# Windowed attention, a rotation mixer and a gated feed-forward on one core: low parts of weights queued later, copies and taps on ScalarE, first loads by two queues

## The chip, the core and the metric

The program runs on one core of a Trainium2 chip. Its engines work side by side, each through its own list of instructions in order: TensorE (PE in the profile, its weight loads PEld), VectorE (DVE), ScalarE (ACT), GpSimd (POOL) and SyncE (SP), which issues most transfers. An instruction that needs another engine's result waits on a semaphore, and all that stands behind it on its own engine waits with it. The metric is the device time of one execution in microseconds, the median of the runs shown. The cost of the host is not in it.

## The reference

```python
# attention, 2 batches x 8 heads, 768 positions, 64 wide
scores = q @ k.T / 8 - slope[h] * dist           # dist: |i-j|, or n_local for far global columns
keep   = (j < n_global) | ((0 <= i-j) & (i-j < n_local))      # n_global 8, n_local 96
x      = softmax(where(keep, scores, -1e9)) @ v  # heads side by side: x is 2 x 768 x 512
# rotation mixer
theta  = x @ w_theta                             # 512 x 512
zr, zi = x * cos(theta), x * sin(theta)
y      = w_tok_r @ zr + w_tok_i @ zi             # 768 x 768, over the tokens
u      = x + y
x2     = u + relu(u @ w_ch)                      # 512 x 512
# gated feed-forward
h      = relu(x2 @ w_in)                         # 512 x 1024
c      = conv over tokens of h, 3 taps per channel
out    = (h * sigmoid(c)) @ w_out                # 1024 x 512
```

The six large weights arrive in 64-bit floating point, everything else in 32 bits.

## The kernel before, in words

The program first reads n_global and n_local and takes one of two branches. With these inputs it is `run_fast`, whose window fits into 128 previous columns; `run_general` is the other and is not run. `begin` issues the loads of the first pair of heads and builds the distance table before the branch; the flag that decides the branch comes out of the same VectorE work.

**Attention** goes in 48 steps, three for each of the 16 heads, two tiles of 128 query rows in a step. Step j is spread over later steps by fixed lags: scores at j on TensorE (bank S), the reduction that adds the table and takes the maximum at j+1 on VectorE (L316), two exponentials at j+2 on ScalarE (L325), transposes at j+3 (L334, bank PT), their copy to memory at j+4 on ScalarE (L101), the product with v at j+5 (bank O), the normalisation at j+6 on VectorE after each third step. After every second head the 128 new channels of x are transposed (X) and split (xTs). From about step 34 the angles of batch 0 (bank TH, tile t at a time) run between the steps.

**Weights.** A weight of 384 or 512 columns passes through six jobs that `weight` makes: a load into one of three (later five) buffers, `a` (one ScalarE operation, L117), `b` (two VectorE operations, L122 and L123), `c` (two more, L129 and L130), which make a 32-bit number of the 64 bits, `d` (the high part, a rounding copy on ScalarE, L101) and `e` (the low part, the difference, on VectorE, L109). `advance` puts the jobs of several weights into one list in an interleaved order, and `run(k)` takes the next k from it; where the calls of `run` stand in the program decides when each engine gets them. Every product is made of three: high by high, low by high, high by low.

**Mixing** follows: the angles of batch 1 (TH, S, PT), the rounding of an angle to turns (`reduce_theta`, r), sine and cosine on ScalarE and the products with x on VectorE (`trig`, z, in high and low parts), then the products with the token weights wt, first half of the 768 columns for batch 0 and 1 (from 151 us and 176 us), then the second half (from 202 us and 234 us), while the weights of the second half, w_ch and w_in are converted. `tok_end` adds a bank to x (xT), `u_split` splits the sum (us), `ch` makes u @ w_ch from 259 us, `ff_in` the product with w_in from 301 us, `gate` the taps, the sigmoid and the split g, and `ff_out` the last product from 368 us.

The code is written out in the order in which each engine takes it; no scheduler moves it.

Of the kernel before, what the change touches and what calls it, by code (L numbers as in the profile page):

```python
# [21 lines left out]
P = 128  # L22
# [31 lines left out]
class Net:  # L54
# [111 lines left out]
    def advance(self, n):  # L166
        j = self.jobs

        def put(i, *steps):
            if 0 <= i < len(j):  # L170
                self.bg.extend(j[i][x] for x in steps)

        put(n - 3, 5)
        put(n - 1, 1)
        put(n - 2, 2, 3)
        put(n, 0)
        put(n - 2, 4)
# [49 lines left out]

def pad_q(nc, t):
    nc.gpsimd.memset(t[D:P, S + KK : QK], 0.0)
    nc.vector.memset(t[0:D, 0:S], 0.0)  # L230
# [172 lines left out]
class Mix:  # L403
# [64 lines left out]
    def reduce_theta(self, th, out):  # L468
# [3 lines left out]
        nc.scalar.activation(out, th, AF.Copy, scale=1.0 / TWO_PI)  # L472
        yield
        nc.vector.tensor_scalar(t, out, MAGIC, -MAGIC, op0=ALU.add, op1=ALU.add)
        nc.vector.tensor_tensor(out, out, t, op=ALU.subtract)

    def trig(self, b, t, r, z, em, eh, el):
# [5 lines left out]
        nc.scalar.activation(r, r, AF.Sin, scale=TURN)  # L483
# [95 lines left out]
    def gate(self, b, f, h, c, banks, em, eh, el):  # L579
# [3 lines left out]
        for hf in range(2):  # L583
            nc.scalar.activation(h[:, HALF * hf : HALF * hf + HALF], banks[hf][:, 0:HALF], AF.Relu)
        yield
        nc.vector.tensor_scalar(c, h, cw[:, f, 1:2], None, op0=ALU.mult)
# [28 lines left out]
    def tail(self, early):  # L615
# [56 lines left out]
        tr = [self.trig(1, s, r[s], self.z[1][s], "VV", "VV", "VV") for s in range(NT)]  # L672
# [62 lines left out]
        for step in (n.f64_a, n.f64_b, n.f64_c):  # L735
            step(n.head["cwb"], n.head["cwt"])
        pipe = Pipe()
        pipe.step(*(self.u_split(0, x, 0, "V", "V") for x in range(KC)))
        for m in range(KC):
# [3 lines left out]
            pipe.step(*(self.u_split(0, x, 1, "V", "V") for x in range(KC) if m == 0))  # L743
# [5 lines left out]

        self.us[1] = [n.slot(t, [P, KC, S], F32R, "us") for t in ("xs0", "y1")]  # L750
# [22 lines left out]
        cs = n.slot("xT1", [P, 4, S], F32, "c")  # L773
# [3 lines left out]
        for k in range(2 * NF):  # L777
# [3 lines left out]
            pipe.step(self.gate(b, f, hs[k % 3], cs[:, k % 4], banks, "V", "A", "V"))  # L781
# [10 lines left out]
def run_fast(tc, net):  # L792
# [4 lines left out]
    att.load_v(0)  # L797
    att.load_v(1)
# [27 lines left out]
    for j in range(NJ + LAG_N + 3):  # L826
# [44 lines left out]
        net.run(1 if j == 0 else 0 if j < 4 else 1 if j < 33 else 3)  # L871
# [4 lines left out]
def run_general(tc, net):  # L876
# [3 lines left out]
    mix = Mix(net, xs)  # L880
    for i in range(NH):
# [51 lines left out]
def begin(nc, io, net, small, head):  # L933
# [6 lines left out]
    for k, q in ((slice(0, 2 * KW), slice(KK, KK + 2 * P)), (slice(2 * KW, KK), slice(KK + 2 * P, KK + S))):  # L940
        nc.sync.dma_start(qk0[0:D, S + k.start : S + k.stop], two[:, k])
        nc.sync.dma_start(qk0[D:P, S + k.start : S + k.stop], one[:, S + k.start : S + k.stop])
# [75 lines left out]
```

## Time and profile before

| | |
|---|---|
| runs of the kernel before | 438.99, 438.33 and 2325.94 us, median 438.99 |
| the profiled execution, whole | 441.24 us |
| its span, first to last instruction | 439.0 us |
| mean granted TensorE clock | 0.988 |
| busy: TensorE, VectorE, ScalarE, GpSimd | 413.4, 342.9, 203.6, 2.9 us |
| read from memory, written | 34.39 MB, 3.15 MB |

The profile gives one execution. A group line names the code line, engine, operation, what it writes and reads and its shape, then busy time, the mean time of one and the idle time before it with the engine that ended it. A bracket in a timeline row is the same for one instruction. Matmuls are pipelined: a record begins when the array takes it up and ends by a model, so the distance from one begin to the next is the better measure of pace. A granted clock of 1.00 is 2.4 GHz and 0.50 is 1.2 GHz.

### The profile page before, as it was taken

The numbers are of one execution on the slowest core, as the hardware profiler recorded it, in microseconds if no ns is written. First come the engines' busy times: TensorE is split into PE (matmuls) and PEld (weight loads), VectorE is DVE, ScalarE is ACT, GpSimd is POOL, SyncE is SP. The second block draws the span as 40 slices with busy tenths as digits, with TensorE's granted clock in tenths as the row PEclk, the third lists the DMA queues.
The fourth block names the chain that finished last, engine by engine and source line by source line (L and its number), as shares of the span: only waits on it lengthen the run. The fifth ranks groups of instructions, "written<-read, shape, count | busy, mean of one in ns | idle before, by whom it ended". The sixth has DMA issues, their size and how long they took to land.

```text
span 439.0 us, 6394 instructions
## 1 busy us (share of the span) xinstructions
PE 413.4 (94%) x2376; PEld 383.4 (87%) x2376; DVE 342.9 (78%) x783; ACT 203.6 (46%) x401; POOL 2.9 (1%) x12
## 2 busy tenths in 40 slices
PE   4799999999999999999879998699999999999995
PEld 3699999988897899999669998499999999888885
DVE  4458877977788998997879988999999999980001
ACT  2467777675668414702332233544554445530000
POOL 2000000000000000000000000000000000000000
PEclk9889999999999999999999999989999999999999
DMA  5946565372410014004454234222000000002111
GB/s 161 249 142 179 144 160 150 110 216 73 167 47 1 0 30 116 1 6 139 134 166 145 96 107 141 97 88 88 9 0 2 0 2 0 1 33 110 49 48 55
DMA packets 13096, 38.04 MB, mean 87 GB/s; under 512 B 1856, under 2 KB 2304, under 8 KB 13056
## 3 DMA queue, kind: packets, MB, share of 16 engines
q1 hardware_dynamic: 13056, 37.54, 29.1%
q8 instruction: 20, 0.33, 0.3%
q14 instruction: 20, 0.16, 0.1%
HBM read 34.39 MB, written 3.15 MB: 86 GB/s over the span
## 4 chain that ended last, share of the span: by engine, by line
PE 61%; DVE 30%; ACT 3%; DMA 2%; SPq 2%; issue 1%; ACTq 0%; DVEq 0%
PE O L112 18%; PE S L112 16%; PE TH L112 8%; PE PT L112 8%; PE X L112 5%; PE PT L334 4%; DVE wbit L129 4%; DVE wbit L130 4%; DVE z L109 3%; DVE wbit L123 3%; DMA wst<-w_theta 2%; DVE wbit L122 2%; DVE wt L109 2%; DVE z L105 2%; ACT wt L101 2%; DVE r L488 2%
## 5 line engine op out<-in xcount | busy, mean ns | idle before, releaser
L112 PE MATMUL S<-qk 128*128 128x256 f32 (+1 forms) x192 | 50.9, 394 | 6.6 <-DVE nnl L981 5.8
L316 DVE CUSTOM_DVE_ANT_0 a<-S,a 128x256 f32<-128x256 f32 (+1 forms) x96 | 34.9, 398 | 23.1 <-PE PT L334 15.7
L325 ACT ACTIVATE a<-a,nm 128x256 f32<-128x256 f32 (+1 forms) x96 | 41.4, 480 | 11.0 <-DVE nm L316 11.0
L112 PEld LDWEIGHTS S<-qk 128*128 128x128 f32 x192 | 33.8, 205 | 10.7 <-issue 7.3
L101 ACT ACTIVATE wt<-wbit 128x384 fp32r<-128x384 f32 x24 | 12.5, 523 | 52.1 <-DVE wbit L130 52.1
L112 PE MATMUL O<-wt,z 128*128 128x384 f32 x144 | 29.2, 342 | 5.3 <-ACT wt L101 5.3
L101 ACT ACTIVATE a<-PT 128x512 f32<-128x512 f32 (+1 forms) x48 | 26.6, 553 | 15.4 <-PE PT L334 15.0
L112 PEld LDWEIGHTS O<-wt,z 128*128 128x128 f32 x144 | 24.8, 188 | 7.9 <-ACT wt L101 6.5
L112 PE MATMUL O<-a,a 128*128 128x65 f32 x236 | 31.1, 276 | 0.0
L112 PEld LDWEIGHTS O<-a,a 128*128 128x128 f32 x236 | 30.2, 200 | 0.0
L334 PE MATMUL PT<-ident,a 128*128 128x128 f32 x176 | 27.9, 279 | 2.3 <-ACT a L101 2.3
L334 PEld LDWEIGHTS PT<-ident,a 128*128 128x128 f32 x176 | 22.8, 145 | 7.5 <-ACT a L101 2.7
L112 PE MATMUL PT<-wt,z 128*128 128x384 f32 x144 | 28.1, 335 | 0.0
L112 PE MATMUL S<-wt,z 128*128 128x384 f32 x144 | 26.5, 336 | 0.5 <-DVE z L109 0.5
L112 PEld LDWEIGHTS S<-wt,z 128*128 128x128 f32 x144 | 25.1, 188 | 0.8 <-DVE z L109 0.8
L112 PE MATMUL TH<-wth,xTs 128*128 128x512 f32 x96 | 25.9, 406 | 0.0
L112 PEld LDWEIGHTS PT<-wt,z 128*128 128x128 f32 x144 | 25.3, 188 | 0.0
L109 DVE TENSOR_TENSOR wt<-wbit,wt 128x384 fp32r<-128x384 f32 x24 | 13.4, 557 | 11.5 <-ACT wt L101 11.2
L117 ACT ACTIVATE wbit<-wst 128x384 f32<-128x384 f32 (+1 forms) x33 | 19.9, 602 | 4.8 <-DMA wst<-w_theta 4.8
L130 DVE SCALAR_TENSOR_TENSOR wbit<-wst,wbit 128x384 int32<-128x384 int32 (+1 forms) x33 | 20.6, 623 | 1.1
L129 DVE SCALAR_TENSOR_TENSOR wbit<-wst,wbit 128x384 int32<-128x384 int32 (+1 forms) x33 | 20.5, 622 | 0.9
L123 DVE TENSOR_SCALAR wbit<-wbit 128x512 int32<-128x512 int32 (+1 forms) x48 | 18.9, 394 | 1.6
(179 smaller groups left out, 868.6 us busy)
## 6 DMA issues: line engine op xcount, KB each, us to landing
wst<-w_tok SPq DMA_DIRECT2D x17, 384.0 KB, 3.1
a<-v SPq DMA_DIRECT2D x16, 357.5 KB, 3.9
qk<-qk SPq DMA_DIRECT2D x14, 396.0 KB, 5.5
out<-scratch SPq DMA_DIRECT2D x11, 256.0 KB, 2.0
qk<-w_tok SPq DMA_DIRECT2D x7, 384.0 KB, 3.1
wst<-w_out SPq DMA_DIRECT2D x5, 512.0 KB, 3.5
wst<-w_theta SPq DMA_DIRECT2D x4, 512.0 KB, 9.5
qk<-w_in SPq DMA_DIRECT2D x4, 512.0 KB, 3.5
```

The lines of the kernel that those rows point to most:

```text
L101: self.nc.scalar.activation(out, in_, AF.Copy)
L105: self.nc.vector.tensor_copy(out, in_)
L109: e.tensor_tensor(out, in_, hi.bitcast(F32), op=ALU.subtract)
L112: self.nc.tensor.matmul(out, l, r, start=start, stop=stop)
L117: self.nc.scalar.activation(t.bitcast(F32), w[:, 1 : w.shape[1] : 2].bitcast(F32), AF.Abs)
L122: nc.vector.tensor_scalar(t.bitcast(F32), t.bitcast(F32), F64_LOW, F64_HIGH, op0=ALU.max, op1=ALU.min)
L123: nc.vector.tensor_scalar(t, t, 3, 0x3FFFFFFF, op0=ALU.logical_shift_left, op1=ALU.bitwise_and)
L129: nc.vector.scalar_tensor_tensor(t, lo, 29, t, op0=ALU.logical_shift_right, op1=ALU.bitwise_or)
L130: nc.vector.scalar_tensor_tensor(t, hi, -(1 << 30), t, op0=ALU.bitwise_and, op1=ALU.bitwise_or)
L316: nc.vector.tensor_tensor_reduce(sS[:, c], s["sp"][:, c], self.T[i % H][:, 256:TW] if t0 else self.T[i % H][:, 0:256], scale=-0.125, scala ...
L325: self.nc.scalar.activation(sS[:, rng[u]], sS[:, rng[u]], AF.Exp, bias=nm[:, u : u + 1], scale=-1.0)
L334: self.nc.tensor.transpose(pt[:, c], sS[:, c], net.head["ident"])
```

## The change

Six things are altered; the matmuls and their order are the same on TensorE.

1. In `advance` the low part of weight n-3 is put behind the bit operations of weight n-2, where it stood ahead of them.
2. In the attention loop the first load of weights is taken at step 3, nothing more until step 9, and then two jobs in each step; before it was one at step 0, one a step from step 4, and three from step 33.
3. The loads of the first pair of heads are cut in two: three are issued by SyncE and three by ScalarE. The seventh (the second head's q, 64x768) is issued after the branch, behind the first load of v. The taps' weights (cwb) are loaded where they are needed, and their conversion stands later.
4. The rounding of an angle is a second ScalarE copy (adding the magic number) and one VectorE operation, where it was two VectorE operations. The result has the other sign, which the sine's scale undoes.
5. The rounding copies for the high part of z in batch 1 and of the first u move from VectorE to ScalarE.
6. The middle tap moves from VectorE to ScalarE, with a fifth buffer for c. The clearing of unused q rows moves from VectorE to GpSimd.

```diff
@@ advance
-        put(n - 3, 5)
         put(n - 1, 1)
         put(n - 2, 2, 3)
         put(n, 0)
+        put(n - 3, 5)
         put(n - 2, 4)
@@ load of the second head's q, and the clearing
+def load_qk_second(nc, io, t):
+    nc.sync.dma_start(t[D:P, 0:S], io["qk"][0, 1][:, 0:S])
...
-    nc.vector.memset(t[0:D, 0:S], 0.0)
+    nc.gpsimd.memset(t[0:D, 0:S], 0.0)
@@ reduce_theta
         nc.scalar.activation(out, th, AF.Copy, scale=1.0 / TWO_PI)
-        yield
-        nc.vector.tensor_scalar(t, out, MAGIC, -MAGIC, op0=ALU.add, op1=ALU.add)
-        nc.vector.tensor_tensor(out, out, t, op=ALU.subtract)
+        nc.scalar.activation(t, out, AF.Copy, bias=MAGIC)
+        yield
+        nc.vector.scalar_tensor_tensor(out, t, -MAGIC, out, op0=ALU.add, op1=ALU.subtract)
@@ gate
-        yield
-        nc.vector.tensor_scalar(c, h, cw[:, f, 1:2], None, op0=ALU.mult)
+        nc.scalar.activation(c, h, AF.Identity, scale=cw[:, f, 1:2])
+        yield
@@ tail
-        tr = [self.trig(1, s, r[s], self.z[1][s], "VV", "VV", "VV") for s in range(NT)]
+        tr = [self.trig(1, s, r[s], self.z[1][s], "VV", "AA", "VV") for s in range(NT)]
...
-        for step in (n.f64_a, n.f64_b, n.f64_c):
-            step(n.head["cwb"], n.head["cwt"])
+        self.nc.sync.dma_start(n.head["cwb"], n.io["conv_w"].bitcast(I32))
...
-        pipe.step(*(self.u_split(0, x, 0, "V", "V") for x in range(KC)))
+        pipe.step(*(self.u_split(0, x, 0, "A", "V") for x in range(KC)))
...
-            pipe.step(*(self.u_split(0, x, 1, "V", "V") for x in range(KC) if m == 0))
+            pipe.step(*(self.u_split(0, x, 1, "A", "V") for x in range(KC) if m == 0))
...
         self.tok_end(1, KC - 1, 1, last)
 
+        for step in (n.f64_a, n.f64_b, n.f64_c):
+            step(n.head["cwb"], n.head["cwt"])
@@ run_fast
     att.load_v(0)
+    load_qk_second(nc, io, att.qk[0])
     att.load_v(1)
...
-        net.run(1 if j == 0 else 0 if j < 4 else 1 if j < 33 else 3)
+        net.run(1 if j == 3 else 0 if j < 9 else 2)
@@ begin
-    for k, q in ((slice(0, 2 * KW), slice(KK, KK + 2 * P)), (slice(2 * KW, KK), slice(KK + 2 * P, KK + S))):
-        nc.sync.dma_start(qk0[0:D, S + k.start : S + k.stop], two[:, k])
-        nc.sync.dma_start(qk0[D:P, S + k.start : S + k.stop], one[:, S + k.start : S + k.stop])
-        nc.sync.dma_start(qk0[0:D, S + q.start : S + q.stop], two[:, q])
-    nc.sync.dma_start(qk0[D:P, 0:S], one[:, 0:S])
+    ks, qs = (slice(0, 2 * KW), slice(2 * KW, KK)), (slice(KK, KK + 2 * P), slice(KK + 2 * P, KK + S))
+    for e, k, q in ((nc.sync, ks[0], qs[0]), (nc.scalar, ks[1], qs[1])):
+        e.dma_start(qk0[0:D, S + k.start : S + k.stop], two[:, k])
+        e.dma_start(qk0[D:P, S + k.start : S + k.stop], one[:, S + k.start : S + k.stop])
+        e.dma_start(qk0[0:D, S + q.start : S + q.stop], two[:, q])
```

Three places of the instruction lists show it. The first is ScalarE just after the branch, steps 2 to 8 of attention; `wbit<-wst` is job `a` of a weight of w_theta, which reads the loaded buffer. Before:

```order
L325 ACTIVATE a_5_134<-a_5_134,nm_176 128x256 x2
L101 ACTIVATE a_3_132<-PT_182 128x384
L117 ACTIVATE wbit_200<-wst_146 128x512
L325 ACTIVATE a_5_134<-a_5_134,nm_189 128x128
L325 ACTIVATE a_5_134<-a_5_134,nm_189 128x256
L101 ACTIVATE a_4_133<-PT_194 128x512
L325 ACTIVATE a_5_134<-a_5_134,nm_205 128x256 x2
L101 ACTIVATE a_5_134<-PT_210 128x512
L117 ACTIVATE wbit_242<-wst_147 128x512
```

And now:

```order
L101 ACTIVATE a_4_131<-PT_193 128x512
L330 ACTIVATE a_5_132<-a_5_132,nm_202 128x256 x2
L101 ACTIVATE a_5_132<-PT_207 128x512
L330 ACTIVATE a_5_132<-a_5_132,nm_223 128x256 x2
L101 ACTIVATE a_3_130<-PT_229 128x384
L330 ACTIVATE a_5_132<-a_5_132,nm_241 128x128
L330 ACTIVATE a_5_132<-a_5_132,nm_241 128x256
L101 ACTIVATE a_4_131<-PT_246 128x512
L330 ACTIVATE a_5_132<-a_5_132,nm_259 128x256 x2
L101 ACTIVATE a_5_132<-PT_264 128x512
L117 ACTIVATE wbit_297<-wst_145 128x512
```

The first job on a weight stood behind the first copy of PT and now stands behind the sixth, with the exponentials of five more steps ahead of it.

The second is VectorE where the conversion of the second half of the token weights begins; `wt` is the low part, job `e`. Before:

```order
L122 TENSOR_SCALAR wbit_1884<-wbit_1884 128x384
L123 TENSOR_SCALAR wbit_1884<-wbit_1884 128x384
L129 SCALAR_TENSOR_TENSOR wbit_1884<-wst_148,wbit_1884 128x384
L130 SCALAR_TENSOR_TENSOR wbit_1884<-wst_148,wbit_1884 128x384
L109 TENSOR_TENSOR wt_1881<-wbit_1884,wt_1881 128x384
L122 TENSOR_SCALAR wbit_1887<-wbit_1887 128x384
```

And now:

```order
L122 TENSOR_SCALAR wbit_1883<-wbit_1883 128x384
L123 TENSOR_SCALAR wbit_1883<-wbit_1883 128x384
L129 SCALAR_TENSOR_TENSOR wbit_1883<-wst_147,wbit_1883 128x384
L130 SCALAR_TENSOR_TENSOR wbit_1883<-wst_147,wbit_1883 128x384
L122 TENSOR_SCALAR wbit_1886<-wbit_1886 128x384
L123 TENSOR_SCALAR wbit_1886<-wbit_1886 128x384
L129 SCALAR_TENSOR_TENSOR wbit_1886<-qk_63,wbit_1886 128x384
L130 SCALAR_TENSOR_TENSOR wbit_1886<-qk_63,wbit_1886 128x384
L109 TENSOR_TENSOR wt_1880<-wbit_1883,wt_1880 128x384
```

Between the last bit operation of a weight and its low part there now stand the four bit operations of the next weight.

The third is ScalarE in the second half of the angles, at the first token tiles of batch 1; abs, sine and cosine of a tile are L487 to L489 now, and `z` the new copies. Before there were none of these copies here:

```order
L482 ACTIVATE scratch<-r_145 128x512
L483 ACTIVATE r_145<-r_145 128x512
L484 ACTIVATE scratch<-scratch,hp 128x512
L482 ACTIVATE scratch<-r_145 128x512
L483 ACTIVATE r_145<-r_145 128x512
```

And now:

```order
L478 ACTIVATE scratch<-r_144 128x512
L487 ACTIVATE scratch<-r_144 128x512
L488 ACTIVATE r_144<-r_144 128x512
L489 ACTIVATE scratch<-scratch,hp 128x512
L487 ACTIVATE scratch<-r_144 128x512
L488 ACTIVATE r_144<-r_144 128x512
L489 ACTIVATE scratch<-scratch,hp 128x512
L101 ACTIVATE z_1647<-r_144 128x512
L101 ACTIVATE z_1647<-scratch 128x512
L487 ACTIVATE scratch<-r_144 128x512
```

The copies of a tile stand behind the sine and cosine of the tile after it.

## Rows read from the trace of the kernel before

**Rows 1.** The page's busy time: engine, share of the span, instructions.

```profile
PE 413.4 (94%) x2376; PEld 383.4 (87%) x2376; DVE 342.9 (78%) x783; ACT 203.6 (46%) x401; POOL 2.9 (1%) x12
```

**Rows 2.** The page's chain of waits, shares of the span by engine.

```profile
PE 61%; DVE 30%; ACT 3%; DMA 2%; SPq 2%; issue 1%; ACTq 0%; DVEq 0%
```

**Rows 3.** Waits of TensorE: for whom, us in total, times, longest.

```profile
PE O L112 <- ACT wt L101: 5.3, 4, 1.8
PE O L112 <- DVE us L109: 4.1, 2, 2.9
PE PT L334 <- ACT a L101: 2.3, 1, 2.3
PE TH L112 <- DVE xT L534: 1.1, 1, 1.1
PE S L112 <- DMA qk<-qk: 0.8, 1, 0.8
PE S L112 <- DVE z L109: 0.5, 1, 0.5
```

**Rows 4.** Windows: stretch, length, busy PE PEld DVE ACT POOL, PEclk, DMA share, GB/s.

```profile
12.10:18.90 6.80, 4.59 (x30) 3.78 (x28) 2.48 (x14) 1.81 (x5) 0.00 (x0) 1.00 1.01 266
18.90:25.70 6.80, 5.90 (x24) 5.43 (x25) 2.36 (x10) 5.22 (x13) 0.00 (x0) 0.50 0.72 192
34.08:46.73 12.65, 12.65 (x99) 11.84 (x98) 10.49 (x40) 9.87 (x23) 0.00 (x0) 1.00 0.60 155
277.60:288.75 11.15, 6.85 (x27) 5.58 (x25) 11.05 (x24) 7.59 (x17) 0.00 (x0) 0.85 0.28 96
301.40:368.60 67.20, 67.20 (x385) 67.20 (x385) 65.56 (x91) 34.80 (x60) 0.00 (x0) 1.00 0.04 12
```

**Rows 5.** Timeline of PE, 15 to 22 us: start, us, line, what, count, [idle before].

```profile
15.02 0.78 PE L112 MATMUL O<-a 128*128 128x65 f32 x6
16.63 0.89 PE L112 MATMUL S<-qk 128*128 128x128 f32 x4 [0.83 <-DMA qk<-qk]
19.80 0.90 PE L334 MATMUL PT<-ident,a 128*128 128x128 f32 x3 [2.28 <-ACT a L101]
```

**Rows 6.** Timeline of ACT in the same stretch.

```profile
17.92 0.66 ACT L117 ACTIVATE wbit<-wst 128x512 f32<-128x512 f32 x1 [4.82 <-DMA wst<-w_theta]
```

**Rows 7.** Timeline of PE at the second half's token products, 202 to 235 us.

```profile
202.13 2.24 PE L112 MATMUL O<-wt,z 128*128 128x384 f32 x12
...
206.29 2.24 PE L112 MATMUL O<-wt,z 128*128 128x384 f32 x12
...
234.50 0.68 PE L112 MATMUL S<-wt,z 128*128 128x384 f32 x3
```

**Rows 8.** Timeline of DVE there: two successive low parts.

```profile
202.83 0.56 DVE L109 TENSOR_TENSOR wt<-wbit,wt 128x384 fp32r<-128x384 f32 x1 [0.59 <-ACT wt L101]
...
205.83 0.56 DVE L109 TENSOR_TENSOR wt<-wbit,wt 128x384 fp32r<-128x384 f32 x1 [0.59 <-ACT wt L101]
```

**Rows 9.** Timeline of PE at the products with w_ch, 277 to 289 us.

```profile
277.64 2.14 PE L112 MATMUL O<-us,wch 128*128 128x384 f32 x7
...
284.64 0.62 PE L112 MATMUL O<-us,wx 128*128 128x384 f32 x2 [2.87 <-DVE us L109]
...
288.75 1.72 PE L112 MATMUL X<-us,wch 128*128 128x384 f32 x9
```

**Rows 10.** Groups by form: mean ns behind the comma; stretches from 138 to 369 us.

```profile
L474 DVE TENSOR_SCALAR scratch<-r 128x512 f32<-128x512 f32 x6 | 2.5, 419 | 0.0
L105 DVE CAST z<-r 128x512 fp32r<-128x512 f32 x12 | 5.0, 416 | 0.0
L105 DVE CAST us<-xT 128x384 fp32r<-128x384 f32 x8 | 2.3, 352 | 0.0
L586 DVE TENSOR_SCALAR c<-scratch,cwt 128x768 f32<-128x768 f32 x12 | 7.4, 616 | 0.2
L101 ACT ACTIVATE wout<-wbit 128x512 fp32r<-128x512 f32 x6 | 3.8, 628 | 8.5 <-DVE wbit L130 8.5
```

More of the change, by code (lines that the diff above doesn't have):

```diff
@@ L482, in trig @@
         nc.scalar.activation(a, r, AF.Abs)
-        nc.scalar.activation(r, r, AF.Sin, scale=TURN)
+        nc.scalar.activation(r, r, AF.Sin, scale=-TURN)
         nc.scalar.activation(a, a, AF.Sin, bias=n.head["half_pi"], scale=-TURN)
@@ L771, in tail @@
         n.drain()
-        cs = n.slot("xT1", [P, 4, S], F32, "c")
+        c4 = n.slot("xT1", [P, 4, S], F32, "c")
+        cs = [c4[:, i] for i in range(4)] + [n.slot("c", [P, S], F32, "c")]
         hs = [n.head["scratch"][:, S * i : S * i + S] for i in range(3)]
@@ L780, in tail @@
             self.ff_in(b, f, banks)
-            pipe.step(self.gate(b, f, hs[k % 3], cs[:, k % 4], banks, "V", "A", "V"))
+            pipe.step(self.gate(b, f, hs[k % 3], cs[k % 5], banks, "V", "A", "V"))
             n.run(4)
@@ L880, in run_general @@
     mix = Mix(net, xs)
+    load_qk_second(nc, io, att.qk[0])
     for i in range(NH):
@@ L939, in begin @@
     two, one = io["qk"][0, 0], io["qk"][0, 1]
-    for k, q in ((slice(0, 2 * KW), slice(KK, KK + 2 * P)), (slice(2 * KW, KK), slice(KK + 2 * P, KK + S))):
-        nc.sync.dma_start(qk0[0:D, S + k.start : S + k.stop], two[:, k])
-        nc.sync.dma_start(qk0[D:P, S + k.start : S + k.stop], one[:, S + k.start : S + k.stop])
-        nc.sync.dma_start(qk0[0:D, S + q.start : S + q.stop], two[:, q])
-    nc.sync.dma_start(qk0[D:P, 0:S], one[:, 0:S])
+    ks, qs = (slice(0, 2 * KW), slice(2 * KW, KK)), (slice(KK, KK + 2 * P), slice(KK + 2 * P, KK + S))
[3 more added lines that the diff above has]
+        e.dma_start(qk0[0:D, S + q.start : S + q.stop], two[:, q])
     pad_q(nc, qk0)
     cwb = small.tile([P, 2 * NF * 3], I32, name="cwb")
-    nc.sync.dma_start(cwb, io["conv_w"].bitcast(I32))
     R = scratch[:, 0:384]
```

## The prediction

> **What bounds the kernel now.** I read the busy time first, then the chain of waits, then what TensorE itself waited for, and last the stretches around each wait. TensorE is busy for 413.4 of 439.0 us [rows 1]. The chain of waits gives VectorE 30% of the span [rows 2], 132 us, nearly all of it in the mixer, which looks like a stage bound by VectorE. It is not quite that. In the second half's token products one token tile, four banks of six matmuls, takes from 202.13 to 206.29, 4.16 us or 173 ns a matmul [rows 7]; the stage with w_in, where TensorE has no gap in 67.20 us and issues 384 matmuls, has 175 ns [rows 4]. So TensorE runs at full pace there too, and VectorE only decides where a wait appears. The order of the matmuls is not altered, hence only gaps and time at the lower clock can be won. The reader is to see six of them in TensorE's waits, 14.1 us together [rows 3], and that pace lost around them makes them dearer than they look.
>
> **The start, 15 to 26 us.** ScalarE stands at job `a` of the first w_theta weight until 17.92, 4.82 us, for its load [rows 6]. Behind it are a copy of PT and the exponentials, and TensorE idles 2.28 us before 19.80 [rows 5]. Then the clock is at 0.50, 1.2 GHz, from 18.90 to 25.70, with TensorE busy 5.90 us in it [rows 4]; at the full level half of that, 2.95, would do. The change takes this job at step 9, when the load is there. Gain 2.28 + 2.95 = **5.2**. Just before, TensorE waits 0.83 for the second pair's q and k [rows 5]. Those loads now stand behind fewer others on SyncE (three have gone to ScalarE, the taps' weights come later), but q of the second head still goes ahead of them, into a stretch where the transfer engines are full (share 1.01, 266 GB/s) [rows 4]. Between nothing and 0.83 I take **0.5**. A new cost: ScalarE's three loads run beside the small load of n_global and n_local, from which the branch hangs. No row shows that; it is nothing if the small one goes first and at most about one wait of the kind just named, 0.83, if not. I take 0.4 lost.
>
> **Attention, steps 9 to 32.** In place of one job a step there are two, so one more weight in six steps. Six steps take 12.65 us on TensorE, VectorE is busy 10.49 and ScalarE 9.87 of it [rows 4]. A weight of 384 columns costs VectorE 3.00 us from one low part to the next, less the wait of 0.59, 2.41 [rows 8]; with 512 columns at most a third more, 3.2. VectorE then has 12.9 to 13.7 us of work for 12.65, for the two times six steps that carry the four wide weights: 0.5 to 2.1 us lost. Two score banks let VectorE run a step late, so I take 0.5. ScalarE gets two more operations of 0.63 [rows 10], 11.1 of 12.65, and covers them. The transfers rise by 0.5 MB in 12.65 us, from 155 to about 196 GB/s, under the 266 reached above [rows 4]. The fewer jobs after step 33 win nothing: TensorE has the angles there and no wait in the list.
>
> **The angles and z, 138 to 202 us.** Six roundings lose one VectorE operation of 0.42 each, 2.5 us; three waits of about 0.6 before low parts [rows 8] go, 1.8; twelve copies of 0.42 go, 5.0 [rows 10]. ScalarE gains six copies for the roundings and twelve for z at 0.63. Per token tile it has five operations, at most 5 x 0.63 = 3.2 us, against 4.16 on TensorE; the low part of z waits for a copy that stands behind the next tile's sine, so VectorE is paced by ScalarE and I count no lead from the twelve copies. The others give VectorE a lead of 2.5 + 1.8 = 4.3 us, and the wait of 0.5 for z [rows 3] goes: **0.5**.
>
> **Second half's token products, 202 to 235 us.** Six tiles at 4.16 need 24.96 us; they take 234.50 - 202.13 = 32.37 [rows 7]. The 7.4 us between are the four waits of 5.3 [rows 3] and the restarts behind them. VectorE is late there: each of twelve weights contains a wait of 0.59 for ScalarE's high part [rows 8]. With the next weight's bit operations (2.41 less 0.56 for the low part, 1.85) between, the high part is done, since ScalarE needs 0.63 for it [rows 10]. At the last weight VectorE is 4.3 + 12 x 0.59 = 11.4 us ahead of where it was; 7.4 suffice. Gain **7.4**. What is late next is xT, which waits for the last product; there VectorE's lead ends and it follows TensorE.
>
> **Products with w_ch, 259 to 301 us.** TH waits 1.1 for xT, O twice for the low part of us, 4.1 [rows 3]. Two units of twelve matmuls begin at 277.64 and the next at 288.75 [rows 9]: 11.11 us for 4.16, so 6.95 lost, with the clock at 0.85 on average [rows 4]. VectorE is relieved of eight copies, 2.3 us [rows 10], of up to 12 x 0.59 in front of the low parts of w_ch and w_in, and of the lag it had at the end of the token products. That is more than the 5.2 it was late. The taps' conversion comes back behind the last xT, four operations on 24 columns, hidden while TensorE works through its eight units for batch 0. Gain 1.1 + 6.95 = **8.05**.
>
> **From 301 us** TensorE is gapless. The tap leaves VectorE, 0.62 [rows 10], and comes to ScalarE at about 0.63 x 768/512 = 0.94, sixteen times, 15 us more on an engine busy 34.80 of 67.20 [rows 4]. Nothing; if TensorE were not in front, the tap would cost 0.3 each. [...]
>
> **The sum.** 5.2 + 0.5 - 0.4 - 0.5 + 0.5 + 7.4 + 8.05 = 20.75. The profiled execution took 441.24, so it becomes 420.5; the median of the runs shown, 438.99, lies 2.25 below it, and the forecast for the median is **418.2**.
>
> **Rivals.** (a) ScalarE becomes what is waited for: low parts of z and of us, and the high parts of weights, are late behind its sines and copies, and half of 7.4 + 8.05 comes back: 426. For it: it gets 48 operations. Against: it is idle for more than half of the span [rows 1]. 0.12. (b) The startup change does not do what it says, because the weights' loads still come late or other loads do: 5.2 stays, 423.4. 0.06. (c) VectorE does pace attention, nearer the upper bound and with ScalarE waiting for loads at steps 12 to 21: 3 to 8 us, 421 to 426. 0.06. (d) The chain of waits is right and VectorE does bound 138 to 301: everything that leaves it counts, 2.5 + 1.8 + 5.0 + 7.1 + 2.3 + 7.1 = 25.8 in place of 15.95, about 408. Against: 173 ns a matmul. 0.03. (e) Slower: with VectorE over its budget in steps 9 to 32 TensorE idles a little in each step and the clock goes to 1.2 GHz there, as it did around the waits before 19.80 and 284.64 [rows 4, 5, 9]. These 24 steps are four times 12.65, 50.6 us of TensorE; wholly at half the pace they cost 50.6 and the time is 469; from 60% of them (30 us) the kernel is slower by 2%. For: the page named next. Against: four waits of up to 1.8 us among the second half's products [rows 3] were not followed by a stretch of half pace: the six tiles there lose 7.4 us in all, little more than the waits. 0.05. The Trainium skill, TensorE: Matmul & The Clock Gate, A second HAM failure mode, says that short idle times between groups of matmuls can make the clock swing between its two levels; the row from 18.90 agrees that it falls after a wait, the four waits of the token products do not.
>
> **How the numbers follow.** The forecast has 0.68, (a) 0.12, (b) 0.06, (c) 0.06, (d) 0.03, (e) 0.05. The range of the forecast alone: without the three losses and with the restart share seen in the token products (7.4 for 5.3) on the other waits, 415.5; with attention at its upper bound and the branch late, 421. Taking in (a), (b) and (c) with 2 us for their bounds it is 415.5 to 428, which leaves out (d), (e) and a little of (a) and (c). Two per cent, 8.8 us, is about what a measurement here tells from no change. Faster than that means under 430.2: the forecast, (b), (d), and most of (a) and (c), 0.90. Within: the rest of them and the mild part of (e), 0.06. Slower: 0.04.
>
> **What would show it.** ScalarE's first weight job near step 9 and no wait above 1 us for w_theta; full clock from about 12 us on; six steps of attention still at 12.65; no wait for wt's high part on VectorE, and six token tiles in 25 us; no wait for us. A wait of TensorE for z or us through ScalarE would make it wrong, as would a clock row at 0.50 between 28 and 82 us or gaps at S in attention.

## The result and the profile after

The kernel after takes 418.52 us (median of 4 runs, 417.66 to 418.75); the kernel before, run beside it, 439.9 (of four too). The ratio is 0.952, 95% interval 0.948 to 0.956. Ratios and intervals here leave out slow runs, those over 1.5% above the fastest of the same kernel, such as the one of 2325.94 us. The forecast was 418.2. The profiled execution took 418.75, with a span of 416.5 against 439.0. The two traces thus differ by 22.5 us; the medians differ by 21.4, or by 20.5 from the 438.99 on which the forecast was built.

The page's busy line and its chain of waits, to be set beside [rows 1, 2]:

```profile
PE 403.7 (97%) x2376; PEld 379.2 (91%) x2376; DVE 318.4 (76%) x733; ACT 236.8 (57%) x449; POOL 4.4 (1%) x14
...
PE 95%; DMA 3%; DVE 1%; SPq 0%; issue 0%; DVEq 0%
```

VectorE has lost 24.5 us of work and ScalarE has taken on 33.2. TensorE's busy time fell by 9.7, though its matmuls are the same 2376: part of that had been half pace (the clock stood at 0.50 for 6.8 us near 19 us and for 3.4 us near 285 us), and the records beside the waits are longer in the trace of before (O<-wt,z 342 ns on average, now 334). The chain of waits, which gave VectorE 30% before, now runs through TensorE nearly from end to end.

What TensorE waits for, in place of [rows 3]:

```profile
PE S L112 <- DMA qk<-qk: 7.2, 2, 6.1
PE X L437 <- DVE xT L105: 0.7, 1, 0.7
```

The 6.1 is the time before the first score product; 1.1 for the second pair's q and k and 0.7 for an xT (there before too) are all that is left. The waits for the high parts of wt, for us, for xT at w_ch, for z and for the copy of PT have gone.

The stretches that answer to [rows 4] are shown next (length, busy PE PEld DVE ACT POOL, PEclk, DMA share, GB/s). They are steps 9 to 14 of attention, steps 21 to 26, the second half's token products for batch 0, the products with w_ch, and those with w_in:

```profile
21.97:34.63 12.66, 12.66 (x99) 11.86 (x98) 10.69 (x39) 10.81 (x25) 0.00 (x0) 1.00 0.69 205
47.28:59.94 12.66, 12.51 (x95) 11.56 (x95) 12.32 (x45) 10.40 (x25) 0.00 (x0) 1.00 0.63 184
195.38:220.34 24.96, 24.96 (x146) 24.96 (x146) 24.06 (x53) 11.29 (x22) 0.00 (x0) 1.00 0.57 181
245.43:278.71 33.28, 33.28 (x193) 33.28 (x193) 32.76 (x70) 17.74 (x36) 0.00 (x0) 1.00 0.29 95
278.71:345.90 67.19, 67.19 (x385) 67.19 (x385) 61.84 (x81) 49.77 (x78) 0.00 (x0) 1.00 0.03 9
```

The third and fourth, where the gaps of [rows 7, 9] lay, have none now on TensorE. VectorE is busy for 96 to 98% of them all the same: it is nearly full there and yet not what is waited for. In steps 21 to 26 it has 12.32 us of work in 12.66, and this is where attention loses a little.

The timelines of TensorE at the start [rows 5] and of ScalarE's first weight job [rows 6]:

```profile
14.02 0.78 PE L112 MATMUL O<-a 128*128 128x65 f32 x6
15.91 0.89 PE L112 MATMUL S<-qk 128*128 128x128 f32 x4 [1.10 <-DMA qk<-qk]
16.64 0.49 PE L339 MATMUL PT<-ident,a 128*128 128x128 f32 x3
```

```profile
22.11 0.68 ACT L117 ACTIVATE wbit<-wst 128x512 f32<-128x512 f32 x1
```

The transposes follow the scores at once, where 2.28 us lay between, and ScalarE's job has no bracket: its load has landed.

VectorE's low parts in the second half [rows 8], then the new or moved groups by form [rows 10]:

```profile
199.75 0.55 DVE L109 TENSOR_TENSOR wt<-wbit,wt 128x384 fp32r<-128x384 f32 x1
...
202.54 0.55 DVE L109 TENSOR_TENSOR wt<-wbit,wt 128x384 fp32r<-128x384 f32 x1
```

```profile
L590 ACT ACTIVATE c<-scratch,cwt 128x768 f32<-128x768 f32 x16 | 15.1, 942 | 0.5
L480 DVE SCALAR_TENSOR_TENSOR r<-scratch,r 128x512 f32<-128x512 f32 x12 | 8.2, 690 | 11.9 <-ACT scratch L478 11.9
L478 ACT ACTIVATE scratch<-r 128x512 f32<-128x512 f32 x12 | 7.6, 632 | 5.6 <-DVE z L109 5.3
L101 ACT ACTIVATE us<-xT 128x384 fp32r<-128x384 f32 x16 | 7.5, 509 | 0.0
```

The bracket of 0.59 has gone from the low parts. A new one has come: VectorE waits 11.9 us in all for ScalarE's rounding (L480). No TensorE wait stands behind it.

Where the time went, by the first matmul of each stage in the two traces:

| stage | before | after | gain | forecast |
|---|---|---|---|---|
| first score product | 5.80 | 6.12 | -0.32 | -0.4 |
| from there to step 4 (first stretch at half pace) | 6.61 | 5.30 | +1.31 | none |
| steps 4 to 6 (wait for the second pair's q and k) | 4.22 | 4.49 | -0.27 | +0.5 |
| steps 6 to 9 (stall, half clock) | 11.40 | 6.06 | +5.34 | +5.2 |
| steps 9 to 47 | 96.74 | 97.13 | -0.39 | -0.5 |
| step 47 to the token products of batch 1 | 51.54 | 51.28 | +0.26 | none |
| token products, first half, batch 1 (z) | 25.82 | 25.00 | +0.82 | +0.5 |
| second half, batch 0 | 32.37 | 24.96 | +7.41 | +7.4 |
| second half, batch 1 | 25.10 | 25.09 | +0.01 | none |
| products with w_ch | 41.63 | 33.28 | +8.35 | +8.05 |
| products with w_in, and all after | as before | | 0.0 | 0 |
| sum | | | 22.5 | 20.75 |

### The profile page after: what moved, and what is told of

Same layout as the page of the kernel before. It is cut to its first block, busy times and chain, and to the rows that moved or that the text cites. A ratio compares the mean times of both kernels' runs of the same rounds, so it can differ in the third digit from the quotient of the medians.

```text
span 416.5 us, 6402 instructions
## 1 busy us (share of the span) xinstructions
PE 403.7 (97%) x2376; PEld 379.2 (91%) x2376; DVE 318.4 (76%) x733; ACT 236.8 (57%) x449; POOL 4.4 (1%) x14
## 4 chain that ended last, share of the span: by engine, by line
PE 95%; DMA 3%; DVE 1%; SPq 0%; issue 0%; DVEq 0%
PE O L112 26%; PE S L112 26%; PE PT L112 16%; PE TH L112 13%; PE X L112 9%; PE PT L339 4%; DMA qk<-qk 2%; PE X L437 1%; DMA words<-n 1%; SPq L258 0%; DVE a L321 0%; DVE xT L105 0%; SPq L224 0%; SPq L230 0%; DVE scratch L105 0%
## 5 line engine op out<-in xcount | busy, mean ns | idle before, releaser
L112 PE MATMUL S<-qk 128*128 128x256 f32 (+1 forms) x192 | 48.7, 380 | 7.4 <-DMA qk<-qk 7.2
L112 PEld LDWEIGHTS S<-qk 128*128 128x128 f32 x192 | 32.6, 198 | 11.1 <-issue 7.6
L101 ACT ACTIVATE a<-PT 128x512 f32<-128x512 f32 (+1 forms) x48 | 26.6, 554 | 11.2 <-PE PT L339 10.8
L112 PE MATMUL O<-a,a 128*128 128x65 f32 x236 | 29.8, 268 | 0.0
L112 PEld LDWEIGHTS O<-a,a 128*128 128x128 f32 x236 | 28.8, 192 | 0.0
L112 PE MATMUL O<-wt,z 128*128 128x384 f32 x144 | 26.9, 334 | 0.0
L129 DVE SCALAR_TENSOR_TENSOR wbit<-wst,wbit 128x384 int32<-128x384 int32 (+1 forms) x33 | 20.5, 622 | 0.9
L112 PEld LDWEIGHTS TH<-wth,xTs 128*128 128x128 f32 x96 | 17.1, 189 | 3.2
```

What stands on the lines that cost most here:

```text
L101: self.nc.scalar.activation(out, in_, AF.Copy)
L112: self.nc.tensor.matmul(out, l, r, start=start, stop=stop)
L129: nc.vector.scalar_tensor_tensor(t, lo, 29, t, op0=ALU.logical_shift_right, op1=ALU.bitwise_or)
```

## The experiments

Twelve kernels were run. Times are medians; ratios are to the kernel before in the same session, so that 0.952 of the kernel after is what they are set against.

**The place of the low parts, undone.**

```diff
+        put(n - 3, 5)
         put(n - 1, 1)
         put(n - 2, 2, 3)
         put(n, 0)
-        put(n - 3, 5)
```

> The kernel after, with the low part of a weight issued ahead of the next block's bit operations again, as before; all else stays moved. Theory (the place of the low part is what made VectorE late, by 0.59 us a weight): the wait for the high part is back on VectorE in every weight, 12 x 0.59 = 7.1 us by the last weight of the second half, less the 2.5 us of the roundings and what of the 5.0 us of copies counts; TensorE waits again in the second half's token products and at w_ch, 425 to 431 us in all. Rival (the copies moved to ScalarE and the fused rounding gave the gain, the order nothing): within 1.5 us of the kernel after, 418.5 to 420. Second rival (the order alone gave all 15.5 us): 434.

Measured: 433.09 us, ratio 0.984 (0.979 to 0.988). Waits of TensorE, then two low parts on VectorE:

```profile
PE O L112 <- ACT wt L101: 4.2, 3, 1.8
PE O L112 <- DVE us L109: 4.1, 2, 2.9
```

```profile
200.39 0.56 DVE L109 TENSOR_TENSOR wt<-wbit,wt 128x384 fp32r<-128x384 f32 x1 [0.59 <-ACT wt L101]
...
206.46 0.56 DVE L109 TENSOR_TENSOR wt<-wbit,wt 128x384 fp32r<-128x384 f32 x1 [0.59 <-ACT wt L101]
```

The wait on VectorE is back at 0.59 and both waits of TensorE with it. The stages give 30.74 us for the second half (5.8 more than after) and 39.47 for w_ch (6.2 more): 12.0 of the 15.8 won there. The other 2.8 of this profile arose before step 9, where TensorE waited 1.8 us for the second pair's q and k and then ran at half clock; up to there each engine has the same operations in the same order as in the kernel after. The 12.0 alone would give 430.5, inside the expected 425 to 431, so what the range missed lies before step 9 in this trace; the other three runs (431.05 to 434.07) were not traced. The first rival falls, since 418.5 to 420 is far off. The second gave 434, near the median, but these stages give 12.0 and not 15.5.

**The place of the low parts alone, in the kernel before** (the same four lines, the other way).

> The kernel before, with only the place of the low part changed. Theory: VectorE gains 0.59 us a weight, 7.1 us by the last weight of the token products, nearly the 7.4 TensorE lost there, and the same again at w_ch and w_in; the waits for wt and us go or shrink below 0.5 each, 14 us less: 425 against 439; the stall at 18 us and its half clock stay. Rival (the copies and roundings are needed as well): half or less, 431 to 435. Rival (order has no effect): 439.

Measured: 425.2 us, ratio 0.965 (0.959 to 0.970). Its four runs spread from 421.6 to 429.3, mean granted clock 1.000 to 0.988, and the ratio is of the three shorter ones (median 424.1); the profile is of the longest, in which TensorE waits 3.9 and 2.8 us before step 9, so only its later stages are read, the second half's batch 0 and w_ch:

```profile
204.26:230.95 26.69, 25.26 (x146) 24.94 (x145) 25.69 (x57) 11.65 (x23) 0.00 (x0) 1.00 0.59 180
256.04:289.32 33.28, 33.28 (x193) 33.28 (x193) 32.80 (x67) 17.62 (x34) 0.00 (x0) 1.00 0.31 98
```

w_ch is at its bound, 33.28, without one copy moved: this one reordering gives all 8.35 there. The second half keeps 1.7 us of its 7.4. Together the order gives 14.0 here, which is the 14 expected, and 425 is met. With the run before this the table is complete: in these two stages all the rest without the order gives 3.8 us, the order without the rest 14.0, and both 15.8.

**Copies, tap and rounding back on VectorE** (order and start as after).

```diff
-        nc.scalar.activation(t, out, AF.Copy, bias=MAGIC)
         yield
-        nc.vector.scalar_tensor_tensor(out, t, -MAGIC, out, ...)
+        nc.vector.tensor_scalar(t, out, MAGIC, -MAGIC, op0=ALU.add, op1=ALU.add)
+        nc.vector.tensor_tensor(out, out, t, op=ALU.subtract)
...
-        nc.scalar.activation(c, h, AF.Identity, scale=cw[:, f, 1:2])
         yield
+        nc.vector.tensor_scalar(c, h, cw[:, f, 1:2], None, op0=ALU.mult)
...
-        ... self.trig(1, s, r[s], self.z[1][s], "VV", "AA", "VV")
+        ... self.trig(1, s, r[s], self.z[1][s], "VV", "VV", "VV")
-        ... self.u_split(0, x, 0, "A", "V")       # and the one with 1
+        ... self.u_split(0, x, 0, "V", "V")
```

> The kernel after, with the copies of u and z, the tap and the rounding back on VectorE; order of the low parts and the start as after. Theory (TensorE is at full pace in these stages and VectorE decides only whether a wait appears; the low parts' place gave the slack): 418.5 to 421, at most the z wait of 0.5 and one of us, below 2 us, return. Rival (the chain of waits is right: VectorE bounds 138 to 301 us, and all that leaves it counts): 2.1 of roundings, 5.0 of z's copies, 2.3 of u's, so 428. Rival (lead at the start of the second half is needed): 3 to 5 us of waits for wt come back, 422 to 424.

Measured: 420.52 us, ratio 0.956 (0.953 to 0.960). TensorE in the second half:

```profile
219.56 1.50 PE L112 MATMUL O<-wt,z 128*128 128x384 f32 x7 [1.41 <-DVE wt L109]
```

One wait of 1.41 us is all that comes back; the six tiles take 26.66, as in the run before this, and w_ch 33.28. It is the wait that the third reading named, for wt, at less than half its size; those for z and us, which the first allowed, do not return. All the moves to ScalarE together are worth about 2 us here, 1.7 of it seen in this stage, not the 10 that the chain of waits would give; the intervals of the two ratios overlap, so the size rests on the trace. The Trainium skill, ScalarE: Activation LUTs, Rules for kernel authors, puts multiplications on VectorE and not on ScalarE. That does not decide in this kernel: the tap takes 942 ns on ScalarE (L590) for 616 on VectorE [rows 10], and costs nothing, since TensorE has no gap in that stage.

**The same, with z's copies on ScalarE** (one line of that edit left out).

> As the run that put copies, tap and rounding back on VectorE (420.5), but the twelve copies of z for batch 1 are on ScalarE again. In that run the six token tiles of the second half took 26.66 us, 1.7 more than in the kernel after, with one wait of 1.4 for the low part of wt. Theory (the forecast: z's copies give VectorE no lead, because it then waits for ScalarE; it is the roundings, 2.5 us, that were missing): the wait of 1.4 stays, 420 to 420.7. Rival (z's copies do give a lead, 5.0 us of work less): no wait, the six tiles at 24.96, 418.8.

Measured: 420.08 us, ratio 0.956 (0.953 to 0.959).

```profile
217.70 1.51 PE L112 MATMUL O<-wt,z 128*128 128x384 f32 x7 [0.72 <-DVE wt L109]
```

Neither theory: the wait halves, and the tiles take 25.98. z's copies give 0.7 us; the 1.0 that is left goes to the fused rounding and the other moves, which were not run apart. The forecast's reading that z's copies give no lead was too strict.

**The old numbers of jobs a step, in the kernel after.**

```diff
-        net.run(1 if j == 3 else 0 if j < 9 else 2)
+        net.run(1 if j == 0 else 0 if j < 4 else 1 if j < 33 else 3)
```

> The kernel after, with the old numbers of weight jobs a step (one at step 0, one a step from step 4 to 32, then three). Theory: ScalarE stands again at the first w_theta weight near step 4 to 5, TensorE idles some 2.3 us and then runs at 1.2 GHz for some 6 to 7 us, so 5.2 us come back: 423.7. The attention loses its 0.4 no more. Rival (the wait goes because fewer loads stand ahead on SyncE, not because the job is taken later): 418 to 419, and no row of the clock at 0.50 near 20 us.

Measured: 423.77 us, ratio 0.964 (0.958 to 0.969). ScalarE, then TensorE:

```profile
17.56 0.66 ACT L117 ACTIVATE wbit<-wst 128x512 f32<-128x512 f32 x1 [4.51 <-DMA wst<-w_theta]
```

```profile
19.44 0.55 PE L339 MATMUL PT<-ident,a 128*128 128x128 f32 x3 [2.38 <-ACT a L101]
```

The stall returns with nearly its length of before (4.82 and 2.28 in [rows 5, 6]), and the clock of 0.50 after it, and the median of 423.77 (421.38 to 425.00) is the 423.7 expected. In this trace steps 6 to 9 lose 4.2 us, not 5.2: half clock lasts 3.4 us here, from 21.25, against 6.8 before. That the time agrees so closely is in part luck.

**The new numbers of jobs a step alone, in the kernel before.**

> The kernel before with only the new numbers of weight jobs a step. Theory: ScalarE takes the first w_theta job at step 9 when its load is there, the stall of 2.28 us and the stretch of half clock go, 5.2 us less: 433.8; a wait for the second pair's q and k of about 1 us stays at step 6, and the waits for wt and us stay at 5.3 and 4.1. Rival (the loads on SyncE in their old order land later, so that the load jobs that now come two a step are the ones waited for): 436 to 439. Second rival (two jobs a step make VectorE late in the angles of the first batch too): 437 or more.

Measured: 436.73 us over 9 runs (434.05 to 439.18), ratio 0.991 (0.988 to 0.994). A wait of TensorE, and the stretch behind it:

```profile
PE S L112 <- DMA qk<-qk: 1.8, 1, 1.8
```

```profile
16.77:20.15 3.38, 3.38 (x15) 3.10 (x16) 0.73 (x4) 1.18 (x3) 0.00 (x0) 0.54 1.08 266
```

ScalarE's stall is gone, as expected, and yet only 3.8 of the 5.2 us is won by the medians (440.5 beside it), with the shortest runs near the 433.8 expected. This profile is of a long run, and between steps 4 and 9 it wins 2.6: TensorE reaches step 6 sooner, waits longer there for q and k (1.79 for 0.83), and the clock falls after that wait. Whether the shorter queue of SyncE helps against this is not shown: in the traces with the loads of the kernel after in their order, the same wait ranges from none to 1.80 us, and where it was 1.75, with the place of the low parts undone, the clock fell as well. The waits for wt and us stay, 3.9 and 4.1, so the start does nothing for them.

**Three jobs a step from step 9** (`else 3` for `else 2`).

> The kernel after, with three weight jobs a step from step 9 in place of two, so that VectorE has more work than a step lasts on TensorE: 1.35 us of its own a step (10.49 less one weight of 2.41 in six steps) and 1.2 to 1.6 of a weight's half, 2.55 to 2.95 against 2.11. Theory of this run (TensorE then waits 0.4 to 0.8 us in each of 24 steps, and keeps 2.4 GHz, since its waits are short): 10 to 20 us more, 428 to 438, and the granted clock 1.00 throughout the attention. Rival (slower case of the forecast: short waits in every step bring the clock to 1.2 GHz): rows of 0.50 between 22 and 80 us, matmuls at twice the time, 440 to 469. Second rival (loads or ScalarE pace the weights, and VectorE is never over its budget for long): 418.5 to 422.

Measured: 424.46 us, ratio 0.965 (0.962 to 0.967). Twelve steps that took 25.69 in the kernel after, in two stretches:

```profile
49.86:64.08 14.22, 13.16 (x98) 12.02 (x98) 13.88 (x50) 11.48 (x28) 0.00 (x0) 1.00 0.71 199
64.08:78.62 14.54, 13.38 (x99) 12.10 (x98) 14.13 (x50) 10.64 (x27) 0.00 (x0) 1.00 0.60 169
```

VectorE has 13.88 and 14.13 us of work for 12.66, and TensorE goes at its pace: six steps take 14.2 to 14.5. Attention loses 4.9 us in all, not 10 to 20; from step 9 to 20 it lost only 1.8, and in the first six of those nothing, with ScalarE waiting 0.98 us for a load. The clock stays at 1.00 throughout, with TensorE's gaps spread over the steps. The Trainium skill, TensorE: Matmul & The Clock Gate, A second HAM failure mode, tells of a kernel in which frequent short idle times made it swing between its levels; this trace does not show that. So the slower case of the forecast has no support in this stage, and the third case, that VectorE can come to pace attention, is shown: two jobs a step are just at its edge.

**The loads of the first head by one queue.**

```diff
-    for e, k, q in ((nc.sync, ks[0], qs[0]), (nc.scalar, ks[1], qs[1])):
+    for e, k, q in ((nc.sync, ks[0], qs[0]), (nc.sync, ks[1], qs[1])):
```

> The kernel after, with all six of the first head's loads issued by SyncE again; ScalarE issues none. The estimate in the sum was that the loads of ScalarE, beside the small load of n_global and n_local, cost 0.4 at the first score product. Theory (they cost it): the first score product starts near 5.8 instead of 6.12 us and the time is 418.0 to 418.5. Rival (the second queue lets q and k land sooner, so it gains): SyncE issues six loads of some 0.6 us one after the other, the last one 1.8 us later than now; score products of step 0 or 1 wait for it, 419.0 to 420.5. Second rival (the length of the first stretch at 1.2 GHz, which differs from run to run by over 1 us, hides both): 418 to 419.5 with runs spread over more than 1 us.

Measured: 419.38 us (418.47 to 419.75), ratio 0.953 (0.951 to 0.956). Its first score product starts at 5.84, 0.28 sooner, as before; step 9 at 22.38, 0.41 later, because the way from that product to step 4, at half pace for longer, takes 5.97 us for 5.30. No product of step 0 or 1 waits for a load, so the rival's number came without its mechanism. With the intervals overlapping, neither a gain nor a loss by the second queue is shown in the time.

Its cost of about 0.3 us at the first product is shown: that product starts at 5.80 to 5.92 in the four profiles with one queue and at 6.08 to 6.33 in the seven with two (leaving out those with extra products on TensorE). The cause is not the one named. Here are the first product on TensorE, the small load of n_global and n_local (`words`), and the time to landing of SyncE's first three loads of q and k, in this run:

```profile
5.84 5.81 PE L112 MATMUL S<-qk 128*128 128x128 f32 x16 [5.84 <-DVE nnl L989]
0.74 2.55 DMA words<-n
DMA to landing us min/median/max: 2.3/2.3/2.3
```

And in the kernel after:

```profile
6.12 5.13 PE L112 MATMUL S<-qk 128*128 128x128 f32 x16 [6.12 <-DMA qk<-qk]
0.74 2.61 DMA words<-n
DMA to landing us min/median/max: 3.3/3.5/3.6
```

The small load is 0.06 us later with two queues, no more. What is late is q and k of the first head: with ScalarE's loads beside them, SyncE's three take 3.3 to 3.6 us for 2.3, and the first product waits for the last of them. (All six loads have landed by 5.98 us with two queues and by 7.07 with one; the first product needs SyncE's three.)

**The second pair's q and k ahead of the second head's v.**

```diff
-    att.load_v(1)
     load_qk(nc, io, att.qk[1], 2)
+    att.load_v(1)
```

> The kernel after, with the load of the second pair's q and k ahead of the second head's v on SyncE. Theory (TensorE's wait of 1.10 us at step 6 is for this load alone, which stands in a queue of full transfers): it lands 1.3 us sooner, the time that 0.36 MB takes at 266 GB/s, the wait goes, 417.4. Rival (the transfers are full and the v that is put back is then waited for at step 3 plus five): the wait turns into one of TensorE at O for v, 418.5. Second rival (a later load, the first w_theta weight, then comes late for ScalarE at step 9): 419 to 421.

Measured: 418.21 us (418.09 to 418.32), ratio 0.951 (0.949 to 0.953). TensorE at step 6:

```profile
14.69 0.78 PE L112 MATMUL O<-a 128*128 128x65 f32 x6
15.30 0.87 PE L112 MATMUL S<-qk 128*128 128x128 f32 x4
```

No bracket: the wait of 1.10 is gone and v is not missed. Step 9 starts 0.62 sooner than in the kernel after, although the first stretch at half pace was longer in this run (step 4 at 12.08 for 11.42). In the median it is 0.3, within the uncertainty, where 1.1 was expected.

**That, and TensorE kept busy before the branch.**

```diff
+    with net.tc.tile_pool(name="warm", bufs=1, space=bass.MemoryType.PSUM) as wp:
+        warm = wp.tile([P, 256], F32, name="warm")
+        nc.vector.memset(scratch[:, 2048:2304], 1.0)
+        for _ in range(6):
+            nc.tensor.matmul(warm, scratch[:, 2048:2176], scratch[:, 2048:2304], start=True, stop=True)
```

> The load of the second pair's q and k ahead of the second head's v, as in the run before (418.2), and six products of 128 by 256 ones on TensorE ahead of the branch, from about 1 us, into a bank that is free; their result is used nowhere. Theory (the first score products run at 1.2 GHz because TensorE has done nothing before; they take 0.63 us each until 9 to 12 us after the span's start, then 0.38, so 1.2 to 2.5 us are lost there): with work from 1 us on the stretch of half pace ends some 4 us sooner, and the score products of steps 1 to 3 run at 0.38; 416.0 to 417.2. Rival (the second pair's q and k do not land sooner, so TensorE waits at step 6 for what it gained): 417.8 to 418.5, with a wait of 1 to 2 us for qk. Second rival (the pause of about 1 us between these products and the first score product undoes it, or they delay the branch): 418.2 or more.

Measured: 417.25 us (416.99 to 417.97), ratio 0.947 (0.945 to 0.949), the fastest of all. TensorE at the start:

```profile
1.19 5.49 PE L950 MATMUL warm<-scratch 128*128 128x256 f32 x12 [1.19 <-DVE hp L969]
6.89 2.92 PE L112 MATMUL S<-qk 128*128 128x128 f32 x12 [0.22 <-POOL qk L234]
...
15.16 0.89 PE L112 MATMUL S<-qk 128*128 128x128 f32 x4 [0.56 <-DMA qk<-qk]
```

The score products run at full pace from the first: twelve records take 2.92 us. Of that gain, 0.77 goes on a later start, and most of what is left is met by loads that have not landed (0.35 us at step 3, 0.56 at step 6): step 9 starts at 21.22, 0.13 sooner than with the reordered loads alone. This profile (417.97) was the longest of its five runs; where the rest of the 1 us lies, by which the median is below that run, no trace shows.

**Nine of them.**

> As the run with six products ahead of the branch, but nine of them: at 0.63 us each they last until about 6.6 us, over the time at which the branch is read and the first score product starts (6.1). Theory (TensorE's reading of the branch comes behind them): the first score product starts 0.5 to 1.5 us later than with six, 416.5 to 418.5. Rival (the clock rises among them, since they go on without a pause, and gives it back): equal to the run with six, or up to 0.5 us faster.

Measured: 417.83 us (417.50 to 418.12), ratio 0.949 (0.947 to 0.951). The first score product starts at 7.72, 1.6 us later than in the kernel after; step 9 starts at 20.72, 1.25 us sooner, and 0.63 sooner than with the reordered loads alone, with no wait for q or k at all. An early start of TensorE alone is thus worth little: at full pace it starts late and still comes to steps 3 and 6 within 0.6 and 1.0 us of the landing of their loads.

**Six of them, with the loads in the order of the kernel after.**

> The kernel after with the six products ahead of the branch alone; the second head's v is loaded ahead of the second pair's q and k as in the kernel after. Theory (step 6 waits for q and k that land near 15.8 us whatever TensorE does before): the wait of 1.10 us at step 6 grows by what the start gains, 418.2 to 418.8. Rival (the transfers, not delayed by anything of TensorE's, were not the limit): 416.5 to 417.5.

Measured: 420.06 us (418.60 to 421.91), ratio 0.955 (0.952 to 0.958).

```profile
PE S L112 <- DMA qk<-qk: 1.5, 1, 1.5
```

The time gained at 1.2 GHz is waited out at step 3, for the second head's q, which landed near 10.7; at step 6, where the wait was expected to grow, 0.44 us is left, put down to VectorE and ended 0.1 us after those loads landed. It even comes out slower than expected: the two longer runs have a mean clock of 0.993 to 0.994 against 0.997 to 0.998 in the shorter, so a fall of the clock after such a wait is likely in them; only the shortest was profiled, and its clock did not fall there.

## Why the prediction was right, and where not

**The bound.** That TensorE paces the mixer and VectorE only decides whether a wait appears was the step on which all rested. It held: after the change the second half runs at 24.96 and w_ch at 33.28 us, both 173 ns a matmul, with VectorE 96 to 98% busy. Putting the work back on VectorE cost 2.0 us (1.7 by the traces) where the chain of waits promised 10.

**Second half and w_ch, 15.45 forecast, 15.76 measured.** The mechanism is shown from both sides: undone, the 0.59 and both waits return; alone, it gives 14.0 of the 15.8. Two sizes were off. The lead that the order gives at the last weight is smaller than the 7.1 us counted, 12 times 0.59: 5.7 of 7.4 were won by it alone. Ten of the twelve low parts carry that wait in the trace of before, 6.0 us together, and two carry none, so "each of twelve weights" was read from too few rows:

```profile
217.90 0.56 DVE L109 TENSOR_TENSOR wt<-wbit,wt 128x384 fp32r<-128x384 f32 x1
...
227.42 0.56 DVE L109 TENSOR_TENSOR wt<-wbit,wt 128x384 fp32r<-128x384 f32 x1
```

And the copies and roundings were needed for the last 1.7, of which z's copies, counted at nothing, gave 0.7.

**The start, 5.2 forecast, 5.34 measured.** That the later job is what ends the stall is shown by the old numbers of jobs in the kernel after. The size is less sure than the match suggests, since it hangs on how long half clock lasts, 6.8 us in the trace of before and 3.4 with the old numbers. What the forecast lacked was its condition: in the kernel before the same edit gives 3.8 us by the medians, and in the traced run the wait for q and k grows to 1.79 us with half clock behind it.

**The step that failed: "between nothing and 0.83 I take 0.5".** The wait grew to 1.10. The load landed at about 15.8 for 16.5 us, but TensorE arrived 0.99 us sooner too. That the change makes it land sooner is not shown: in the six other traces that load in the same order it landed between 15.2 and 16.9. The 1.3 us gained ahead of it, unforeseen, is the first stretch at half pace (its score products begin 0.43 us apart, later 0.21). It ended at 9.5 us in this profile, at 12.1 in that of before, between the two in those of the experiments with the same first loads, and at 10.2 and 10.8 in the two other traces of the kernel before with one edit. It moves by more than 1 us where nothing ahead of it was edited, so it is luck of these two traces and no merit of the change. Without it the traces' sum is 21.2 for the 20.75 forecast: the 0.8 that this term was off is made up by the others, which came out 1.2 larger together. So close a match of the sum is luck as well.

**Attention and the branch.** -0.39 for -0.5, all of it at steps 23 to 25; -0.32 for -0.4. The reason given for the first was incomplete: the steps 9 to 47 take 96.74 us with two jobs a step and the old order of low parts, and 96.74 with the new order and the old numbers, as before; only both together lose 0.39. Why the combination does was not tried further. In the second, the size came true and the mechanism did not: the forecast had the small load of n_global and n_local, and with it the branch, held up by ScalarE's loads, but that load is 0.06 us later, and the first product waits for the first head's own q and k, whose last piece from SyncE takes 1.3 us longer to land after the same issue. The later load of the second head's q and the later taps were not run apart.

**The angles and z.** 0.82 for 0.5; another 0.26 before it, not forecast. The 0.82 needs no rounding on ScalarE, to which the forecast gave 2.5 of the 4.3 us of lead behind this term: the order of the low parts alone gives it (24.99 us for that stage in the kernel before with that edit).

**The rivals.** ScalarE is not waited for by TensorE, though VectorE waits 11.9 us for it. That VectorE paces attention came true for 0.39 us at two jobs a step, and for 4.9 more at three. The case of a clock that falls in attention did not occur after step 9, even where TensorE lost 0.3 us a step. Its argument against, that the four waits among the token products are not followed by half pace, holds in the trace of before but not always: with the new numbers of jobs alone the longest of them is (last section).

## What to carry to other kernels

When two engines hand results back and forth in a pipeline, look on the follower for a short wait that recurs in every item; moving independent operations between producer and consumer removes it, and here that reordering was worth seven times all the work moved to another engine (14.0 us for 2.0). Before an engine that the chain of waits names is relieved, compare the pace per matmul of that stage with that of a stage without gaps: where they are equal, only the waits can be won. At the start of a kernel remove stalls together with the loads behind them, since a stall that goes is met by the next load, and a wait there can cost its own length again in half clock (2.28 us, then 2.95, in the kernel before).

## What the runs showed of the hardware that was not expected

- The clock does not follow the length of a wait alone. After waits for q and k of about 1.8 us near 16 us it fell in two profiles (the old order of low parts, 0.50 from 17.5 to 20.9; the new numbers alone, 0.50 from 17.1 to 20.5) and did not in a third (three jobs a step, 1.00 throughout); after 1.10 us in the kernel after and 0.56 in two others it did not. The same holds among the token products. With the new numbers alone the third wait for wt there is followed by half clock:

```profile
220.78 2.80 PE L112 MATMUL O<-wt,z 128*128 128x384 f32 x9 [1.84 <-ACT wt L101]
221.87:225.28 3.41, 3.41 (x12) 3.41 (x11) 3.15 (x8) 1.09 (x2) 0.00 (x0) 0.50 0.56 202
```

  In the kernel before, the wait of the same length at the same place is not:

```profile
224.44 2.10 PE L112 MATMUL O<-wt,z 128*128 128x384 f32 x9 [1.84 <-ACT wt L101]
222.60:230.00 7.40, 4.71 (x24) 4.09 (x24) 6.24 (x14) 2.17 (x5) 0.00 (x0) 1.00 0.50 167
```

- The first stretch of half pace ended between 9.5 and 12.1 us though TensorE's first product began within 0.6 us in the profiles without extra products. With work from 1.19 us on, it ended near 5.2 and 5.6 us in two profiles and between 6.0 and 6.9 us in a third.
- Three loads issued by a second queue held up those of the first: SyncE's first loads of q and k took 3.3 to 3.6 us to land beside ScalarE's, and 2.3 without them. The small load issued ahead of them landed at 3.35 and 3.29 us.
- A first product that starts 1.6 us later, behind nine extra products, left step 9 0.63 us earlier than with the same loads and none: at full pace TensorE caught up with the loads before step 6.
